# Runs of extra TensorE products behind the last contraction of a two-layer attention and MLP kernel

## The chip, the cores and the metric

The kernel runs on one core of a Trainium2 chip. A core has TensorE (PE in the profile; its loads of the stationary operand are listed as PEld), VectorE (DVE), ScalarE (ACT), GpSimd (POOL) and SyncE (SP), which run beside each other and wait for each other through semaphores. The metric is the device time of one execution, in microseconds, as the median of several runs. Less is better.

## The reference

Four layers in a row, each added to its input: linear attention, MLP, and both again with the same weights. There are 2048 tokens of 640 features.

```python
def _A_ref(x, wqkv, w_phi, wo):
    q, k, v = heads_of(x @ wqkv)                      # H = 32 heads, Dh = 20
    pq = jnp.einsum("bhsd,hdf->bhsf", q, w_phi)
    pk = jnp.einsum("bhsd,hdf->bhsf", k, w_phi)
    phi_q = jnp.concatenate([_softmax(pq), _softmax(-pq)], axis=-1)
    phi_k = jnp.concatenate([_softmax(pk), _softmax(-pk)], axis=-1)
    kv = jnp.einsum("bhsf,bhsd->bhfd", phi_k, v)
    z = jnp.einsum("bhsf->bhf", phi_k)
    o = (phi_q @ kv) / (phi_q . z + 1e-6)
    return o.reshape(B, S, D) @ wo

def _B_ref(x, w1, b1, w2):                            # 640 -> 1536 -> 640
    h = jnp.einsum("bsd,df->bsf", x, w1) + b1
    act = h * jnp.tanh(softplus(h))                   # mish
    return jnp.einsum("bsf,fd->bsd", act, w2)

x = A_x
x = x + _A_ref(_layernorm(x), A_wqkv, A_w_phi, A_wo)
x = x + _B_ref(_layernorm(x), B_w1, B_b1, B_w2)
x = x + _A_ref(_layernorm(x), A_wqkv, A_w_phi, A_wo)
x = x + _B_ref(_layernorm(x), B_w1, B_b1, B_w2)
```

## The kernel before

The tokens are cut into 8 blocks (`NB`) of 256, each two row tiles (`BT` = 2) of 128. Large products are done in float32r: each operand is split into a high part and a low part (names ending in `h` and `l`), and every product becomes three, high x high, high x low and low x high, which accumulate in PSUM. So each factor of a matrix product shows up as three products in the profile, at lines 364 (projections), 759 (first MLP weight) and 801 (second MLP weight). Plain float32 products are used where operands are not split: folding the feature map into the weights (`fold_part`, line 244), the key-value sums (line 436), the averages (line 637). Transposes go through TensorE as well (lines 89, 300 and 608), with the identity `ident`.

A layer has three parts. `attend_first` computes keys, values and queries per block; `attend_second` computes the averages, the output projection and the normalization for the MLP; `dense` is the MLP. The change touches `dense`, in its second and last call (`last` is true).

`dense` walks through 48 steps, 8 blocks times 6 pairs of 128-wide slices of the 1536 hidden features. `hidden` (lines 749 to 765) computes one pair: 30 products with a stationary operand of 128 x 128 from `w1s` and 256 moving columns, into a PSUM tile of the tag `one` (four buffers of 512 columns). `mish` (lines 767 to 785) turns the result into the activation on ScalarE, VectorE and GpSimd and splits it into `ah` and `al`; for the last step it does so in two halves. `contract` (lines 787 to 802) multiplies a pair with the second weight: 24 products with 128 stationary columns from `ah` or `al` and 320 moving columns (`HC` = 320), into PSUM tiles of the tag `mm`. It runs two steps behind `hidden` (`SKEW` = 2), so that the activation has time:

```python
for i in range(len(steps) + SKEW):
    if i < len(steps):
        ...
        acts[i] = hidden(b, pr)
    ...
    if i >= SKEW:
        b, pr = steps[i - SKEW]
        contract(b, pr, *acts.pop(i - SKEW))
        if pr == n_pr - 1:
            end(b)
```

`end` (lines 804 to 829) adds the residual on VectorE. For the last block of the last layer it does so in four pieces of 320 columns (line 811), and sends the output in three transfers from SyncE's queue (lines 813 and 815). Behind that stands only the closing of the program, which the profile puts down to line 959: waits for the engines and transfers, and two rounds in which the engines meet.

The order of each engine's queue comes from a planner that goes by the order of the program text and a simulated timeline; in `dense` nothing is ordered by hand except a few ScalarE instructions (`tc.issue_after`). Instructions of one engine run in the order of its queue. Waits between engines are put in by the framework from what each instruction reads and writes. The line `warm` at the start issues 30 transposes of the identity into a PSUM tile that is not read.

Of the kernel before, what the change touches and what calls it, by code (L numbers as in the profile page):

```python
# [16 lines left out]
P = 128  # L17
# [5 lines left out]
KD = D // P  # L23
# [10 lines left out]
SKEW = 2  # L34
# [7 lines left out]
def kernel(  # L42
# [13 lines left out]
    nc = tc.nc  # L56
# [8 lines left out]
    def mm_tile():  # L65
        return psum.tile([P, 2, 512], F32, tag="mm", name="mm", bufs=2)

    def one_tile():
        return psum.tile([P, 512], F32, tag="one", name="one", bufs=4)
# [10 lines left out]
    def row_block(t, b):  # L80
        return t[b * BLK:(b + 1) * BLK, :].rearrange("(p t) d -> p t d", t=BT)


    ident = const.tile([P, P], F32, name="ident")
# [98 lines left out]
    def load_v_weights():  # L183

        ws = [r1_pair(k) for k in range(KD)]
        for k in range(KD):
            split(ws[k][0][:, D:2 * D], ws[k][1][:, D:2 * D], fetch_v(k))
        return ws
# [77 lines left out]
    def norm_stats(t, xt):  # L266

        bn = work.tile([P, 2, 6], F32, tag="bn", name="bn", bufs=2)
        for c in range(2):
            nc.vector.bn_stats(bn[:, c], xt[:, t, c * HC:(c + 1) * HC])  # L270
        mv = work.tile([P, 2], F32, tag="mv", name="mv", bufs=3)
        nc.vector.bn_aggr(mv, bn)
        return mv

    def norm_scale(b, mvs):

        ve = work.tile([P, BT], F32, tag="ve", name="ve", bufs=2)
        for t in range(BT):
            nc.gpsimd.tensor_scalar(ve[:, t:t + 1], mvs[t][:, 1:2], LN_EPS, 1.0, op0=ALU.add, op1=ALU.mult)
        nc.gpsimd.tensor_tensor(stats[:, b, 0], ve, neg_half, op=ALU.pow)  # L280
        for t in range(BT):
            nc.vector.scalar_tensor_tensor(stats[:, b, 1, t:t + 1], mvs[t][:, 0:1], -1.0,
                                           stats[:, b, 0, t:t + 1], op0=ALU.mult, op1=ALU.mult)
# [32 lines left out]
    def row_tile():  # L316
        return work.tile([P, D], F32, tag="xn", name="xn", bufs=4)
# [9 lines left out]
    def normalize(b, dst, src):  # L327
        for t in range(BT):
            act(dst[t], src[t], AF.Identity, bias=stats[:, b, 1, t:t + 1], scale=stats[:, b, 0, t:t + 1])

    def spill_turned(rows, dst):

        dst = dst.rearrange("(j f) (t q s) -> t q f j s", f=32, t=BT, s=32)
        for t in range(BT):
            nc.vector.transpose(rows[t], rows[t])
            for q in range(4):
                nc.sync.dma_start(dst[t, q], rows[t][32 * q:32 * q + 32].rearrange("f (j s) -> f j s", s=32))

    def load_turned(src, tiles):

        cols = []
        for c, make in zip(range(0, KD, 2), tiles):
            n = min(2, KD - c)
            cols.append(make()[:, :n * BLK].rearrange("p (k s) -> p k s", k=n))
            nc.sync.dma_start(cols[-1], src[c * P:(c + n) * P].rearrange("(k p) s -> p k s", p=P))
        return Transposed(cols=cols)
# [55 lines left out]
    def fetch(x_src, b, xt=None):  # L402
        xt = x_tile() if xt is None else xt
        nc.sync.dma_start(xt, row_block(x_src, b))
        return xt
# [339 lines left out]
    def dense(x_src, x_dst, w1s, w2s, first, last):  # L745
# [41 lines left out]
        def contract(b, pr, ah, al):  # L787
            if pr == 0:
                blocks[b][2] = [mm_tile() for _ in range(BT)]
            pys = blocks[b][2]  # L790
            order = [(t, j) for t in range(BT) for j in range(2)]
            if b == NB - 1 and pr == KF // 2 - 1:
                order = [(t, j) for j in range(2) for t in range(BT)]
            for t, j in order:
                sl = slice(t * P, (t + 1) * P)
                f = 2 * pr + j
                for c in range(2):
                    cs = slice(c * HC, (c + 1) * HC)
                    wh, wl = w2s[f][0][:, cs], w2s[f][1][:, cs]
                    for n, (l, r) in enumerate(((ah, wh), (ah, wl), (al, wh))):  # L800
                        nc.tensor.matmul(pys[t][:, c, :HC], l[:, j, sl], r,  # L801
                                         start=(f == 0 and n == 0), stop=(f == KF - 1 and n == 2))

        def end(b):
            xt, _, pys = blocks.pop(b)
            dst = row_block(x_dst, b)
            if last and b == NB - 1:
                for t in range(BT):
                    for c in range(2):
                        cs = slice(c * HC, (c + 1) * HC)  # L810
                        nc.vector.tensor_tensor(xt[:, t, cs], pys[t][:, c, :HC], xt[:, t, cs], op=ALU.add)  # L811
                        if t == BT - 1:
                            nc.sync.dma_start(dst[:, t, cs], xt[:, t, cs])
                    if t < BT - 1:
                        nc.sync.dma_start(dst[:, t], xt[:, t])
                return
            mvs = []
            for t in range(BT):
                nc.vector.tensor_tensor(xt[:, t, :].rearrange("p (c d) -> p c d", c=2), pys[t][:, :, :HC],
                                        xt[:, t, :].rearrange("p (c d) -> p c d", c=2), op=ALU.add)  # L820
                if not last:
                    mvs.append(norm_stats(t, xt))
            if not last:
                norm_scale(b, mvs)
            nc.sync.dma_start(dst, xt)
            if not last:
                xn = [row_tile() for _ in range(BT)]
                normalize(b, xn, [xt[:, t, :] for t in range(BT)])
                spill_turned(xn, n2_d[b])

        ahead = [None] * BT

        def fetch_rows_of(b):
            for t in range(BT):
                ahead[t] = row_tile()
                nc.sync.dma_start(ahead[t], row_block(x_src, b)[:, t, :])
# [4 lines left out]
        acts = {}  # L841
        nxt = kv_ws = None
        for i in range(len(steps) + SKEW):
            if i < len(steps):
                b, pr = steps[i]
                if pr == 0 and b + 1 < NB:
                    fetch_rows_of(b + 1)
                if pr == 2 and b + 1 < NB:
                    blocks[b + 1] = [fetch(x_src, b + 1), None, None]
                if pr == 3 and (b + 1 < NB or not last):  # L850
                    nxt = load_turned(n1_d[b + 1] if b + 1 < NB else n2_d[0], (v_tile, v_tile, row_tile))
                acts[i] = hidden(b, pr)
                if pr == 1 and b + 1 < NB:
                    with tc.issue_after(exps[0]):
                        normalize(b + 1, ahead, ahead)
                    spill_turned(ahead, n1_d[b + 1])
                if b == 0 and pr == n_pr - 2:
                    with tc.issue_after(exps[0]):
                        nxt.step()
                if pr == n_pr - 1 and (b + 1 < NB or not last):  # L860
                    if b + 1 < NB:
                        blocks[b + 1][1] = nxt
                    with tc.issue_after(exps[0]):
                        nxt.all()
            if i <= KD:
                with tc.issue_after(exps[0]):
                    w = next(last_w2)
                if i:
                    w2s[6 + i] = w
            if i == len(steps) - 1 and not last:  # L870
                with tc.issue_after(exps[0]):
                    kv_ws = load_v_weights()
            if i >= SKEW:
                b, pr = steps[i - SKEW]
                contract(b, pr, *acts.pop(i - SKEW))
                if pr == n_pr - 1:
                    end(b)
        return nxt, kv_ws

    with tc.block(schedule_with_timeline_sim=True):  # L880
        src, first = x, None
        for layer in range(LAYERS):
            last = layer == LAYERS - 1
# [4 lines left out]
            w1s = []  # L888
# [29 lines left out]
            def begin_dense():  # L918
                return normed(0, x1t[0])

            begun = attend_second(src, x1_d, acc, [lambda s=s: fetch_step(*s) for s in steps],
                                  [lambda s=s: make_step(*s) for s in steps], fetch_dense, begin_dense)
            first = dense(x1_d, dst, w1s, w2s, [x1t[0], begun, None], last)
            src = dst

# [37 lines left out]
```

## Time and profile before

| | us |
|---|---|
| median of 2 runs | 1377.49 |
| lowest, highest | 1376.79, 1378.2 |
| span of the profiled execution, first to last instruction | 1375.0 |

The profile is one execution recorded by the hardware. Its page lists busy time by engine, the chain of work that ended last, and the costliest groups of instructions. A group reads: line, engine, operation, output <- inputs, shapes (for TensorE rows x stationary columns, then the moving operand), the count, then busy time in us and the mean ns of one record, then idle time before them with the releaser. A timeline row reads: start in us, length in us, engine, line, operation, and how many were merged. The records of products overlap, since one drains while the next streams.

The groups of the three large product lines and of the activation's slowest instruction:

```profile
L801 PE MATMUL mm<-r2h,ol 128*128 128x320 f32 x1280 | 305.0, 309 | 0.0
L785 POOL TENSOR_TENSOR ol<-big,ol 128x512 fp32r<-128x512 f32 (+1 forms) x98 | 129.9, 1326 | 483.7 <-ACT ol L784 409.3
L759 PE MATMUL one<-xtl,r1h 128*128 128x256 f32 x960 | 268.2, 279 | 0.0
...
L364 PE MATMUL mm<-r1h,xth 128*128 128x320 f32 x600 | 187.6, 313 | 1.6 <-DVE r1l L251 1.6
```

### The profile page before, as it was taken

How to read it: one execution, taken by the hardware profiler on the slowest of the kernel's cores; microseconds unless marked ns; L12 is line 12 of the kernel's file. 1: busy time of each engine (PE TensorE's matmuls, PEld its weight loads, DVE VectorE, ACT ScalarE, POOL GpSimd, SP SyncE). 2: the span in 40 equal slices, each digit the busy share in tenths (PEclk: the TensorE clock that was granted, in tenths of full speed). 3: DMA queues.
4: the chain of work that ended last, by engine and by line, in shares of the span. 5: the costliest groups of instructions: out<-in, count | busy, mean ns of one | idle time of the engine just before them, and what ended most of it. 6: DMA issues, size and time to landing. Idle time of an engine off the chain costs nothing.

```text
span 1375.0 us, 30860 instructions
## 1 busy us (share of the span) xinstructions
PE 1362.1 (99%) x12896; PEld 1349.8 (98%) x12896; DVE 1073.3 (78%) x1822; ACT 581.3 (42%) x970; POOL 441.0 (32%) x334
## 2 busy tenths in 40 slices
PE   9999999999999999999999999999999999999998
PEld 8999999999999999999999999999999999999998
DVE  5898877886688887788769899988678776677775
ACT  4344443222454545545444334332235444454443
POOL 1345553354322222122235434444242111111112
PEclk9999999999999999999999999999999999999999
DMA  9443424788614442244473433368975221333200
GB/s 337 148 95 62 75 40 96 204 242 292 224 55 97 116 105 77 59 107 99 141 245 77 85 59 64 67 132 270 285 253 151 77 59 41 94 97 96 69 29 20
DMA packets 350469, 169.85 MB, mean 124 GB/s; under 512 B 287209, under 2 KB 323801, under 8 KB 350329
## 3 DMA queue, kind: packets, MB, share of 16 engines
q1 hardware_dynamic: 350329, 167.88, 45.2%
q8 instruction: 101, 1.65, 0.5%
q14 instruction: 39, 0.32, 0.1%
HBM read 104.92 MB, written 62.91 MB: 122 GB/s over the span
## 4 chain that ended last, share of the span: by engine, by line
PE 96%; DMA 1%; DVE 1%; ACT 0%; issue 0%; DVEq 0%; SPq 0%
PE mm L364 29%; PE one L759 24%; PE mm L801 24%; PE one L364 12%; PE mm L637 3%; PE one L300 2%; PE one L436 2%; DMA v<-in_wv 1%; DMA r1l<-wp_d 0%; DVE r1l L251 0%; DVE bn L270 0%; ACT xn L129 0%; DVE r L397 0%; DVE xt L811 0%; ACT r L129 0%
## 5 line engine op out<-in xcount | busy, mean ns | idle before, releaser
L801 PE MATMUL mm<-r2h,ol 128*128 128x320 f32 x1280 | 305.0, 309 | 0.0
L785 POOL TENSOR_TENSOR ol<-big,ol 128x512 fp32r<-128x512 f32 (+1 forms) x98 | 129.9, 1326 | 483.7 <-ACT ol L784 409.3
L759 PE MATMUL one<-xtl,r1h 128*128 128x256 f32 x960 | 268.2, 279 | 0.0
L759 PE MATMUL one<-xth,r1l 128*128 128x256 f32 x960 | 268.0, 279 | 0.0
L759 PE MATMUL one<-xth,r1h 128*128 128x256 f32 x960 | 265.9, 279 | 0.0
L801 PEld LDWEIGHTS mm<-r2h,ol 128*128 128x128 f32 x1280 | 219.2, 188 | 0.3 <-ACT ol L784 0.3
L801 PE MATMUL mm<-r2l,ol 128*128 128x320 f32 x640 | 197.3, 309 | 0.0
L364 PE MATMUL mm<-r1h,xth 128*128 128x320 f32 x600 | 187.6, 313 | 1.6 <-DVE r1l L251 1.6
L364 PE MATMUL mm<-r1l,xth 128*128 128x320 f32 x600 | 185.8, 310 | 0.0
L364 PE MATMUL mm<-r1h,xtl 128*128 128x320 f32 x600 | 185.6, 310 | 0.0
L759 PEld LDWEIGHTS one<-xtl,r1h 128*128 128x128 f32 x960 | 180.4, 188 | 0.0
L759 PEld LDWEIGHTS one<-xth,r1l 128*128 128x128 f32 x960 | 180.4, 188 | 0.0
L759 PEld LDWEIGHTS one<-xth,r1h 128*128 128x128 f32 x960 | 179.6, 188 | 0.0
L774 DVE TENSOR_SCALAR big<-big 128x512 f32<-128x512 f32 (+1 forms) x98 | 57.1, 583 | 110.0 <-ACT big L772 109.8
L399 POOL TENSOR_TENSOR r<-r,r 128x1280 f32<-128x1280 f32 x32 | 77.7, 2429 | 156.4 <-DVE r L398 141.8
L801 PEld LDWEIGHTS mm<-r2l,ol 128*128 128x128 f32 x640 | 120.2, 188 | 0.0
L776 ACT ACTIVATE big<-big,two 128x512 f32<-128x512 f32 (+1 forms) x98 | 70.1, 716 | 116.1 <-DVE big L775 116.0
L772 ACT ACTIVATE big<-one,b1s 128x256 f32<-128x256 f32 x192 | 80.9, 468 | 89.0 <-PE one L759 88.5
L784 ACT ACTIVATE ol<-big 128x512 fp32r<-128x512 f32 (+1 forms) x98 | 60.9, 622 | 136.0 <-DVE big L783 135.9
L364 PEld LDWEIGHTS mm<-r1h,xth 128*128 128x128 f32 x600 | 112.8, 188 | 2.6 <-DVE r1l L251 1.8
L364 PEld LDWEIGHTS mm<-r1h,xtl 128*128 128x128 f32 x600 | 112.7, 188 | 0.2
L364 PEld LDWEIGHTS mm<-r1l,xth 128*128 128x128 f32 x600 | 112.8, 188 | 0.0
(133 smaller groups left out, 3119.9 us busy)
## 6 DMA issues: line engine op xcount, KB each, us to landing
e_d<-r SPq DMA_DIRECT2D x128, 160.0 KB, 4.0
big<-e_d SPq DMA_DIRECT2D x32, 640.0 KB, 7.6
x_d<-xt SPq DMA_DIRECT2D x23, 640.0 KB, 3.9
xt<-x_d SPq DMA_DIRECT2D x22, 640.0 KB, 5.5
n_d<-xn SPq DMA_DIRECT2D x176, 80.0 KB, 2.2
xt<-in_x SPq DMA_DIRECT2D x16, 640.0 KB, 4.4
xn<-x_d SPq DMA_DIRECT2D x28, 320.0 KB, 4.4
v<-n_d SPq DMA_DIRECT2D x30, 256.0 KB, 3.1
```

The lines of the kernel that those rows point to most:

```text
L300: nc.tensor.transpose(ps[:, c, t * P:(t + 1) * P], self.rows[t][:, (c0 + c) * P:(c0 + c + 1) * P], ident)
L364: nc.tensor.matmul(ps[:, :HC], a[:, sl], r, start=(k == 0 and n == 0), stop=(k == KD - 1 and n == 2))
L399: nc.gpsimd.tensor_tensor(eg, eg, r.unsqueeze(2).to_broadcast([P, 2 * H, DH]), op=ALU.mult)
L436: nc.tensor.matmul(kva[32 * j:32 * j + DH + 1, 40 * r:40 * r + 40], v[:, (DH + 1) * h:(DH + 1) * (h + 1)], e[:, 40 * h:40 * h + 40], start ...
L637: nc.tensor.matmul(po[64 * q:64 * q + 64, c, GW * j:GW * j + w], phs[g][:n, s0:s0 + 64], kvb[:n, g, :w], start=True, stop=True)
L759: nc.tensor.matmul(ph[:, j, :], l, r, start=(n == 0), stop=(n == 3 * KD - 1))
L772: exps[0] = nc.scalar.activation(part(ta, 0)[:, j - js.start], ph[:, j, :], AF.Exp, bias=b1s[:, 2 * pr + j:2 * pr + j + 1]).ins
L774: nc.vector.tensor_scalar_min(e, e, E_CAP)
L776: nc.scalar.activation(r, n, AF.Ln, bias=two)
L784: nc.scalar.activation(ah[:, js], n, AF.Copy)
L785: nc.gpsimd.tensor_tensor(al[:, js], n, ah[:, js].bitcast(F32), op=ALU.subtract)
L801: nc.tensor.matmul(pys[t][:, c, :HC], l[:, j, sl], r, start=(f == 0 and n == 0), stop=(f == KF - 1 and n == 2))
```

## The change

A new function `widths` in `dense` issues 168 products on TensorE; it is called once, behind the loop, in the last layer. It takes `ah` and `al` of the last step, 128 columns of either as the stationary operand (`sides`), and columns from 512 on of the first MLP weight as the moving operand. It writes two PSUM tiles of the tag `one`. Nothing reads them, and the output is what it was. `contract` gets the same operands as before through two names.

```diff
+        def widths(ah, al):
+
+            ps = [one_tile() for _ in range(2)]
+            sides = (ah[:, 0, :P], al[:, 0, :P], ah[:, 1, :P], al[:, 1, :P])
+            for w in (512, 480, 384, 320, 256, 192, 128, 64):
+                for n in range(12):
+                    nc.tensor.matmul(ps[0][:, :w], sides[n % 4], w1s[n % KD][n % 2][:, 512:512 + w],
+                                     start=(n == 0), stop=(n == 11))
+            for n in range(12):
+                nc.tensor.matmul(ps[1][:, :320], sides[0], w1s[n % KD][n % 2][:, 512:832],
+                                 start=(n == 0), stop=(n == 11))
+            for n in range(12):
+                nc.tensor.matmul(ps[1][:64, :320], sides[n % 4][:, :64], w1s[n % KD][n % 2][:, 512:832],
+                                 start=(n == 0), stop=(n == 11))
+            for n in range(12):
+                nc.tensor.matmul(ps[1][:32, :320], sides[n % 4][:, :32], w1s[n % KD][n % 2][:, 512:832],
+                                 start=(n == 0), stop=(n == 11))
+            for n in range(12):
+                nc.tensor.matmul(ps[n % 2][:, :320], sides[n % 4], w1s[n % KD][n % 2][:, 512:832],
+                                 start=True, stop=True)
+            for n in range(12):
+                nc.tensor.matmul(ps[0][:, :64], ident, ident[:, 64 * (n % 2):64 * (n % 2) + 64],
+                                 start=(n == 0), stop=(n == 11))
+            for n in range(12):
+                nc.tensor.matmul(ps[0][:, :128], ident, ident, start=(n == 0), stop=(n == 11))
...
-                contract(b, pr, *acts.pop(i - SKEW))
+                ah, al = acts.pop(i - SKEW)
+                contract(b, pr, ah, al)
                 if pr == n_pr - 1:
                     end(b)
+        if last:
+            widths(ah, al)
         return nxt, kv_ws
```

So there are eight runs of 12 products with 512, 480, 384, 320, 256, 192, 128 and 64 moving columns; then four runs of 12 at 320 columns, one with a single stationary operand, one with 64 stationary columns, one with 32, and one in which every product starts and ends its own sum; and two runs of 12 in plain float32 with the identity as both operands, at 64 and at 128 columns.

## The prediction

> **What bounds the kernel now.** I read the page first: the span, the busy shares and the chain of work that ended last.
>
> ```profile
> span 1375.0 us, 30860 instructions
> PE 1362.1 (99%) x12896; PEld 1349.8 (98%) x12896; DVE 1073.3 (78%) x1822; ACT 581.3 (42%) x970; POOL 441.0 (32%) x334
> ...
> PE 96%; DMA 1%; DVE 1%; ACT 0%; issue 0%; DVEq 0%; SPq 0%
> ```
>
> TensorE is busy for 99% of the span and carries 96% of the chain. The change adds work at one place only, so next I read the chain in order of time over the last 46 us; these are its last pieces.
>
> ```profile
> 1352.87 3.52 PE mm L801 x24
> 1356.39 3.50 PE one L759 x30
> 1359.89 9.99 PE mm L801 x68
> 1369.88 0.02 issue
> 1369.90 0.89 DVE xt L811 x2
> 1370.79 0.40 DVEq L959
> 1371.18 0.40 DVE xt L811
> ```
>
> Products are issued without a gap to the end. The 68 of the last contraction take 9.99 us, 146.9 ns each; the 24 before them 3.52 us, 146.7 ns. The 30 products 256 wide take 3.50 us, 116.7 ns. These prices are from start to start. A record is longer than that (0.31 us for a product 320 wide, below), because one product drains while the next streams, so a sum of records would count the time twice.
>
> Last comes the tail, in the timeline of the final 5 us and in the view of the closing instructions (line 959, with their first and last start).
>
> ```profile
> 1369.90 1.69 DVE L811 TENSOR_TENSOR xt<-mm,xt 128x320 f32<-128x320 f32 x4 [3.53 <-PE mm L801]
> ...
> 1370.14 0.31 PE L801 MATMUL mm<-r2h,ol 128*128 128x320 f32 x1
> 1370.82 0.34 SPq L815 DMA_DIRECT2D out<-xt  x1
> 1371.21 0.92 SPq L813 DMA_DIRECT2D out<-xt  x2
> ```
>
> ```profile
> L959 SPq EVENT_SEMAPHORE  x7: 17/28/28, 1373.9 to 1374.9; - x7
> ```
>
> TensorE's last product starts at 1370.14 and ends at 1370.45. Then VectorE adds the residual, three transfers go out, SyncE's first closing wait is over at 1373.9, and the kernel ends 1.1 us later, at 1375.0. So TensorE is idle for the last 4.55 us. The profiled span is 1375.0 us; the median of the two runs is 1377.49 us, 2.49 us more, which lie outside the first and last instruction. I carry a difference of spans over to the median unchanged.
>
> **The change, part by part.** Nothing is removed, and no transfer, VectorE or ScalarE work is added. The diff adds, behind the last contraction, 12 products for each of eight widths (96), then four runs of 12 that are 320 wide (48), all with float32r operands, and 24 products of plain float32 (12 at 64 columns, 12 at 128). They read `ah` and `al` of the last step, the first MLP weight and the identity, all of which lie in SBUF by then. They write two tiles of the tag `one`, which nobody reads. No new wait for another engine arises: the last reader of `one` tiles is the last activation, which the last contraction needs anyway. They stand behind the contraction on TensorE's queue, so neither the residual adds nor the output transfers wait for them. What they cost is TensorE's time, minus what the tail hides.
>
> Widths 512 to 256: 146.7 ns at 320 columns and 116.7 ns at 256 are 0.458 and 0.456 ns a column. I take 0.458. The widths 512, 480, 384, 320 and 256 are 1952 columns: 894 ns for one product of each. A straight line through the two points would give 898 ns, which changes the sum by 0.05 us.
>
> Widths 192, 128 and 64: The trace has no float32r product below 256 columns. Below some width the product no longer hides the load of the next stationary operand. What a load costs is seen where plain float32 products are narrow (timeline of the weight folding), and in the weight loads grouped by shape:
>
> ```profile
> 31.72 0.83 PE L244 MATMUL mm<-big,raw 120*128 120x120 f32 x6
> 32.39 0.83 PE L244 MATMUL one<-big,raw 120*128 120x120 f32 x6
> 33.06 0.58 PE L244 MATMUL mm<-big,raw 120*128 120x120 f32 x4
> 33.47 0.39 PE L244 MATMUL mm<-big,r 80*128 80x80 f32 x2
> 33.70 0.61 PE L244 MATMUL one<-big,raw 120*128 120x120 f32 x4
> ```
>
> ```profile
> L801 PEld LDWEIGHTS mm<-r2h,ol 128*128 128x128 f32 x1280 | 219.2, 188 | 0.3 <-ACT ol L784 0.3
> ...
> L759 PEld LDWEIGHTS one<-xtl,r1h 128*128 128x128 f32 x960 | 180.4, 188 | 0.0
> ...
> L759 PEld LDWEIGHTS one<-xth,r1h 128*128 128x128 f32 x960 | 179.6, 188 | 0.0
> ...
> L637 PEld LDWEIGHTS mm<-kvb,big 120*64 120x64 f32 x1280 | 40.0, 138 | 3.9 <-PE one L300 1.7 <-PE mm L637 1.0 <-issue 0.8
> ...
> L436 PEld LDWEIGHTS one<-big,v 128*21 128x21 f32 x2048 | 21.8, 101 | 4.0 <-issue 3.3 <-POOL r L389 0.8
> L244 PEld LDWEIGHTS mm<-big,raw 120*128 120x128 f32 x48 | 6.1, 191 | 2.5 <-DMA raw<-in_wqk_t 1.1 <-DVE r1l L251 1.1 <-issue 0.4
> ```
>
> Six records 120 wide take 0.67 us (31.72 to 32.39, and again to 33.06), 112 ns each; two that are only 80 wide take 0.23 us, 115 ns each. A third fewer columns bring nothing: this is a floor, and it is the load of 128 stationary columns. The load records agree in size: 138 ns for 64 columns and 188 to 191 ns for 128, so 64 columns more cost 50 to 53 ns, and 128 some 100 to 106 ns. The float32r loads (L801, L759) take 188 ns, the same as plain float32 (191 ns), so I give float32r the same floor: 112 ns for each of the widths 192, 128 and 64, 336 ns together. Lower bound: no floor, 0.458 ns a column, 384 columns, 176 ns together. Upper bound: the price of a plain float32 product, in the rivals. All eight widths cost 894 + 336 = 1230 ns, twelve times 14.76 us.
>
> The Trainium skill (TensorE: Matmul & The Clock Gate, section Back-to-back issue gap) gives the distance of warm products as N / 2.4 + 2.5 ns with a lowest value near 25 ns, and no floor from the load. By it the eight widths would take an estimated 11.9 us instead of 14.76. The trace differs from it at 320 columns: 146.7 ns against the estimate of 135.8.
>
> Four runs of 320: Each product keeps its 320 columns, so 146.7 ns: 48 of them, 7.04 us. With 64 or 32 stationary columns the load is shorter, and it was hidden already. One stationary operand for twelve products saves nothing, because L759 shows it: the products with `xth` and `xtl` share one stationary operand (`r1h`) and follow each other, yet each has its own load, 960 and 960. Were that load left out, nothing would be gained either, since it is hidden. A product that starts and ends its own sum costs as one that accumulates. Bounds: 2.7 us more, if the 24 loads with few columns were not hidden and each cost a full 112 ns. None of it less, since the stream of 320 columns remains. I take zero, since the 128-column loads of L801 (1280 in the row above) are hidden behind products of just this width.
>
> Plain float32: A product becomes two records here. L436 has 2048 of them for 32 heads x 16 row tiles x 2 layers = 1024 products. Each record costs at least the load, 112 ns. A stream of 128 columns fits under it, as the transposes show:
>
> ```profile
> 1017.30 1.25 PE L300 MATMUL one<-ident,xn 128*128 128x128 f32 x10
> ```
>
> (1.25 - 0.27) / 9 = 109 ns, taking 0.27 us as one record. So both widths cost 2 x 112 ns: 24 products, 48 records, 5.38 us. Lower bound: 64 columns stream in 54 ns, if their loads were hidden: 1.4 us less.
>
> Sum: 14.76 + 7.04 + 5.38 = 27.18 us on TensorE. The slot behind the last contraction opens at 1370.14 + 0.147 = 1370.29. The last record starts one slot (0.112) before 1397.47, at 1397.36, and ends 0.275 us later (the length of a 112 ns record in the timeline: 0.83 - 5 x 0.112), at 1397.63. The residual adds and the output transfers, over at 1373.9, lie wholly under the new products. The closing then waits for TensorE and not for the transfers: at most the 1.1 us it took before, less the waits that are met already; I take 1.0. Span 1398.6, 23.6 us more than 1375.0. Forecast: 1377.49 + 23.6 = 1401.1 us, 1.7% slower. The clock stays as it is: the last contraction ran at the full granted clock (1.00), and the added products leave no gap in which it could fall.
>
> ```profile
> 1359.89:1369.88 9.99, 9.99 (x70) 9.99 (x70) 5.11 (x12) 3.54 (x8) 2.47 (x3) 1.00 0.01 2
> ```
>
> The cover is 4.55 us of TensorE's idle time at the end, of which 1.0 us returns as closing. Without it the change would cost the whole 27.2 us, 2.0%.
>
> **The rivals.**
>
> Narrow float32r goes at the price of plain float32: The place is the widths below 256 columns. For it: the kernel shows float32r at 256 and 320 columns only, never below. Against it: whether an instruction is one record or two is fixed when the program is built, and float32r is one record everywhere. Price: two records each, at 112 ns for 64 and 128, and at 192 columns a stream of 192 x 109 / 128 = 164 ns, 327 ns a product. That is 327 + 224 + 224 = 775 instead of 336 ns, 5.3 us more in all: 1406.4 us, slower by 2.1%. It decides the sign from 3.9 us more than my sum on, for 2% of 1377.49 is 27.5 us, which is about what a measurement of this kernel can tell from no change. A weaker form, one record that takes twice the transposes' time a column (2 x 0.85 ns: 327, 218 and, by the load, 112 ns), costs 3.9 us more, 1405.0, just on that bound. I give both 13%.
>
> No floor: loads are hidden below 256 columns too: For it: 128-column loads vanish wholly at 256 and 320 columns. Against it: the 112 and 115 ns above. Then the three widths cost 176 ns, 1.9 us less: 1399.2; with the 64-column float32 products also at their stream, 1397.8. I give it 12%. The Trainium skill (same page, section Weight-path perf modes) says that a fast weight load acts on 128 weights whose type is not FP32, which would be such a case if float32r did not count as FP32. The trace speaks against that here, with the equal 188 and 191 ns.
>
> The products are dropped, because nobody reads them: Then nothing changes: 1377.5. Against it stand 30 products at the start that nobody reads either and that are all in the trace:
>
> ```profile
> L89 PE MATMUL one<-ident 128*128 128x128 f32 x30 | 5.1, 350 | 1.3 <-POOL ident masks.py:199 1.3
> ```
>
> I give it 2%. The planner could also put some of them earlier, in a gap of TensorE; since the first four need the last `ah` and `al`, at most a few could move, and a product costs the same time on a full queue wherever it stands.
>
> **How the numbers follow.** The forecast, 1401.1 us, has 73%, with a range of its own from 1399.5 to 1403.5 (1.4 us less for float32 at 64 columns, most of the 2.7 us more for unhidden loads). The rivals have 13, 12 and 2%. The range 1398 to 1406.5 leaves out only the dropped products and the far ends. Faster by over 2% has no mechanism: 1%. Slower by over 2% needs 1405.0: the first rival in its stronger form, part of the weaker one, and unhidden loads on top of something else: 12%. Within 2%: 87%.
>
> **What would show it.** The chain of waits should end in TensorE's new lines, and the closing should follow them by about 1 us; the output transfers should land over 20 us before the end. In the timeline, twelve products should take 2.8 us at 512 columns, 1.76 at 320, 1.4 at 256, and 1.34 at each of 192, 128 and 64. If the times fall below 256 with the width, there is no floor; if 192 takes 2.6 us or more, the first rival holds, and two records for one product would prove its stronger form. The two plain float32 runs should be 24 records each in 2.7 us, alike at 64 and 128. The runs with 64 and 32 stationary columns should equal the 320 run; a longer one would mean loads that aren't hidden. The forecast is wrong if earlier stages differ in their order by more than the 1 us by which runs differ, or if the granted clock falls in the added stretch.

## The result, and the profile after

The changed kernel takes 1400.66 us in the median of two runs (1399.2 and 1402.12), against 1377.49 before: a ratio of 1.0162 with a 95% interval from 1.0125 to 1.0199. The forecast was 1401.1. As a difference from the kernel before, the two medians give 23.2 us, and 23.6 were forecast. The page of the profiled execution, which is the run of 1402.12 us, shows TensorE's work grown by 28.7 us and the other engines' unchanged (VectorE 1073.3 before, 1074.2 after):

```profile
span 1400.3 us, 31244 instructions
PE 1390.8 (99%) x13088; PEld 1377.2 (98%) x13088; DVE 1074.2 (77%) x1822; ACT 581.3 (42%) x970; POOL 441.4 (32%) x334
```

TensorE has 192 more records: 144 products in float32r with one each and 24 in plain float32 with two each. The chain of waits, in order of time, near the last contraction (the rest of it is the new lines):

```profile
1358.35 3.50 PE one L759 x30
1361.85 7.63 PE mm L801 x52
1369.48 0.23 PE one L837
1369.70 1.46 PE one L840 x10
...
```

Two things are to be seen here. First, the last 30 products of line 759 start at 1358.35 and not at 1356.39 as before, so 1.96 us of the longer span arose before any added product ran. From that point to the end it is 1400.3 - 1358.35 = 41.95 us, against 1375.0 - 1356.39 = 18.61 before: the change itself costs 23.3 us. Second, the planner did not leave all of the new products behind the contraction. One of 512 columns and ten of the run with a single stationary operand stand between its 52nd and 53rd product.

The timeline gives the price of each run, as the distance between the first products of one run and the next; the run of 512 columns is taken from its second product behind the contraction (line 837 is the run of widths; line, stationary columns and moving columns are in each row):

```profile
1374.17 0.39 PE L837 MATMUL one<-r1h,ol 128*128 128x512 f32 x1
...
1376.49 0.38 PE L837 MATMUL one<-r1h,ol 128*128 128x480 f32 x1
...
1379.14 0.34 PE L837 MATMUL one<-r1h,ol 128*128 128x384 f32 x1
...
1381.23 0.31 PE L837 MATMUL one<-r1h,ol 128*128 128x320 f32 x1
...
1382.99 0.28 PE L837 MATMUL one<-r1h,ol 128*128 128x256 f32 x1
...
1384.41 0.25 PE L837 MATMUL one<-r1h,ol 128*128 128x192 f32 x1
...
1385.73 0.24 PE L837 MATMUL one<-r1h,ol 128*128 128x128 f32 x1
...
1387.04 0.24 PE L837 MATMUL one<-r1h,ol 128*128 128x64 f32 x1
...
1388.35 0.39 PE L840 MATMUL one<-r1h,ol 128*128 128x320 f32 x1
```

| moving columns | us for the run | ns a product | forecast, ns |
|---|---|---|---|
| 512 | 2.32 for 10 | 232 | 235 |
| 480 | 2.65 | 221 | 220 |
| 384 | 2.09 | 174 | 176 |
| 320 | 1.76 | 147 | 147 |
| 256 | 1.42 | 118 | 117 |
| 192 | 1.32 | 110 | 112 |
| 128 | 1.31 | 109 | 112 |
| 64 | 1.31 | 109 | 112 |

Down to 256 columns a product costs its width, and from 192 down it costs the same. The three last values are somewhat low because the first distance in such a run is only 79 to 86 ns; this returns at the next wide product, where the first distance is 0.22 us, at 1388.35. Inside these runs the distance is 112 ns.

The other 1.96 us lie for the most part in the middle of the program. The wait between the two layers, near 702 us, is also in the kernel before. In this execution it is 0.87 and 0.64 us long (brackets: idle time before, and what ended it):

```profile
702.60 0.41 PE L801 MATMUL mm<-r2h,ol 128*128 128x320 f32 x1 [0.87 <-ACT ol L784]
...
704.10 0.71 PE L364 MATMUL one<-r1h,xth 128*128 128x320 f32 x3 [0.64 <-ACT r1h L137]
```

After it, the view of stretches (busy time of each engine with records in brackets, then TensorE's granted clock) shows a lower clock from 704.5 to 708.5 us. In the changed kernel:

```profile
704.50:708.50 4.00, 4.00 (x19) 4.00 (x18) 3.64 (x7) 1.09 (x2) 1.55 (x1) 0.57 0.20 49
```

The same stretch in the kernel before:

```profile
704.50:708.50 4.00, 4.00 (x29) 4.00 (x28) 4.00 (x10) 0.76 (x2) 1.57 (x1) 1.00 0.47 140
```

A mean of 0.57 over 4 us fits 3.4 us at 0.5. TensorE issued 19 records there instead of 29, ten fewer at 147 ns, 1.5 us; the rest of the 1.96 us are waits that are a few tenths longer. Up to the 53rd product of the last contraction the queues of all engines hold the same instructions in the same order in both kernels.

### The profile page after: what moved, and what is told of

It is laid out like the page before. It is cut to its first block, busy times and chain, and to the rows that moved or that the text cites. A ratio compares the mean times of both kernels' runs of the same rounds, so it can differ in the third digit from the quotient of the medians.

```text
span 1400.3 us, 31244 instructions
## 1 busy us (share of the span) xinstructions
PE 1390.8 (99%) x13088; PEld 1377.2 (98%) x13088; DVE 1074.2 (77%) x1822; ACT 581.3 (42%) x970; POOL 441.4 (32%) x334
## 4 chain that ended last, share of the span: by engine, by line
PE 96%; DVE 1%; DMA 0%; ACT 0%; issue 0%; DVEq 0%; ACTq 0%
PE mm L364 28%; PE one L759 24%; PE mm L801 24%; PE one L364 11%; PE mm L637 3%; PE one L300 2%; PE one L436 2%; PE one L837 1%; DMA v<-in_wv 0%; PE one L855 0%; DVE r1l L251 0%; PE one L852 0%; DVE bn L270 0%; PE one L840 0%; PE one L849 0%
```

## The experiments

Each is the changed kernel with one edit, unless it says otherwise. Since executions of one kernel differ by up to 5 us, the chip's median is given with its interval, and beside it a second measure from the profile that leaves out whatever happened earlier: the time from the start of the last 30 products of line 759 to the end of the span. It was 18.61 us before and 41.95 after.

**The changed kernel again.** No edit.

> The changed kernel once more, unaltered, to settle its distance from the kernel before. The added products take 27.09 us on TensorE in its first profile, 3.7 us of it lie in time in which TensorE was idle anyway. Theory A (products by the row prices, minus the cover; the slip of 2.0 us in the middle of the first profile, where the granted clock was 0.5 for 3.4 us, is a matter of the single run): 23.4 us over before, between 22 and 24, and the kernel before shows runs with such a slip as well. Theory B (the slip comes with the change): 25.3 us over before in nearly all runs.

Median of five runs 1403.01 us (1399.95 to 1403.73), against 1377.95 for 15 runs of the kernel before; ratio 1.0177 (1.0163 to 1.0191), 25.1 us. In the profile, a run of 1399.95 us, the last part starts at 1356.18 and the span is 1398.2: 42.0 us, the same as in the first profile. This profile holds no records of the granted clock, so that a 1.00 in its views says nothing; but TensorE has 29 records from 704.5 to 708.5 us, as in the kernel before, so the slow stretch is not there. So the end of the kernel repeats to a tenth of a microsecond, and the run to run difference lies earlier. The mean granted clock that is recorded with each run points the same way: of the seven runs of the changed kernel, the four with 0.999 took 1402.1 to 1403.7 us and the three with 1.0, this one among them, took 1399.2 to 1400.8 (a stretch of 3.4 us at 0.5 lowers the mean by 0.0012). The median fits theory B, the fastest runs theory A; this run alone does not decide between them.

**All of it behind the contraction.** `done[0]` is the last product that `contract` issued.

```diff
-            widths(ah, al)
+            with tc.issue_after(done[0].ins):
+                widths(ah, al)
```

> All added products are held behind the last product of the contraction; in the first profile the planner had put 11 of them, 1.7 us, into the contraction. Theory A (a product costs the same wherever it stands on a full queue, and the residual adds and output transfers are under cover either way): the same time as the changed kernel within 0.5 us, while the residual adds and transfers start 1.7 us earlier. Rival (their place in the contraction cost or saved time): 1.7 us away from it.

Median of four runs 1400.29 us (1399.19 to 1400.66); ratio 1.0158 (1.0144 to 1.0172). Its chain of waits:

```profile
1356.55 3.50 PE one L759 x30
1360.05 10.56 PE mm L801 x72
1370.61 14.63 PE one L837 x96
1385.24 1.84 PE one L840 x12
1387.08 1.73 PE one L843 x12
1388.82 1.74 PE one L846 x12
1390.56 1.76 PE one L849 x12
1392.33 2.62 PE one L852 x24
1394.95 2.73 PE one L855 x24
```

The contraction runs through in 10.56 us, and its end is at 14.1 us after the start of line 759's last products, 1.7 us earlier than in the changed kernel. The end of the kernel is unmoved: 1398.5 - 1356.55 = 41.95 us. So the planner's placing cost nothing and saved nothing, as theory A has it. The two medians, 1400.29 here and 1403.01 for the changed kernel, do differ by 2.7 us; that lies ahead of the last part, where one of these four runs has a mean clock of 0.999 and three of those five do. These rows also give the other runs: 144 ns a product with 64 stationary columns (line 843), 145 with 32 (line 846), 147 when each product starts and ends its own sum (line 849), 109 and 114 ns a record in plain float32 at 64 and 128 columns (112 inside both runs). The sum of the seven rows of added products is 27.05 us.

**Plain float32 alone.** The runs in float32r are left out, the rest stands behind the contraction.

```diff
-            for w in (512, 480, 384, 320, 256, 192, 128, 64):
...
+            with tc.issue_after(done[0].ins):
+                widths(ah, al)
```

> Of the added products only the 24 in plain float32 are kept, 5.4 us of TensorE's time, held behind the contraction. Theory A (the tail covers 3.7 us): 1.7 us over before, the span ends 0.84 us behind the last product. Rival (no cover, every added product lengthens the kernel in full): 5.4 us over before. Rival (cover of the whole idle 4.55 us): 0.8 us over.

Median of eleven runs 1378.93 us (1377.42 to 1381.95); ratio 1.0011 (1.0002 to 1.0019), 1.0 us. In its profile (span 1377.0 us):

```profile
1356.79 3.50 PE one L759 x30
...
1370.85 2.62 PE one L835 x24
1373.48 2.73 PE one L838 x24
```

From 1356.79 to 1377.0 it is 20.2 us, 1.6 more than before, for 5.35 us of products. So 3.7 us were covered by the tail; no cover at all would have been 5.4. The chip's median, 1.0 with an interval from 0.3 to 2.6 us, also excludes that, and leaves the 0.8 us of the third theory open; the profile's 1.6 decides for theory A.

**Ahead of the last contraction.** The products run before the last call of `contract`, with the activation of the step before.

```diff
+                if last and i == len(steps) + SKEW - 1:
+                    with tc.issue_after(done[0].ins):
+                        widths(ah, al)
                 ah, al = acts.pop(i - SKEW)
...
-        if last:
-            widths(ah, al)
```

> The same 168 products stand ahead of the last contraction, with the activation of the step before as the stationary operand, so that the residual adds and the output transfers follow them as they follow the contraction before. Theory A (the cover is the tail): the full 27.1 us over before, 3.7 us more than the changed kernel. Rival (the end is set by TensorE's sum alone): the same as the changed kernel within 0.5 us.

Median of four runs 1403.53 us (1402.72 to 1406.12); ratio 1.0186 (1.0172 to 1.02), 25.6 us. In the profile (span 1404.3 us) the contraction comes last again, with the tail behind it:

```profile
1358.95 3.50 PE one L759 x30
...
1396.56 2.66 PE mm L801 x18
...
```

From 1358.95 to 1404.3 it is 45.35 us, 26.7 more than before, for 27.1 us of products, and 3.4 more than in the changed kernel. On the chip it is 3.2 us over the run with all products behind the contraction, but only 0.5 over the median of the changed kernel (1403.01), which by itself would fit the rival; the lowest runs, 1402.72 and 1399.95, are 2.8 us apart. The last part of the profile, free of what differs earlier, decides for theory A. So the same products cost 23.3 us behind the contraction and 26.7 ahead of it: the cover is the tail. Of the expected 27.1 us 0.3 are missing; by the profile they are in the closing, behind TensorE's last product.

**What the floor is.** The 14 runs give way to runs with fewer stationary columns.

```diff
+            for m in (128, 96, 64, 32):
+                for w in (128, 64):
+                    for n in range(24):
+                        nc.tensor.matmul(ps[0][:m, :w], sides[n % 4][:, :m], w1s[n % KD][n % 2][:, 512:512 + w],
+                                         start=(n == 0), stop=(n == 23))
...
```

> In place of the 14 runs of the change stand runs of 24 float32r products with 128, 96, 64 and 32 stationary columns, at 128 and at 64 moving columns, then one at 64 with a single stationary operand, and two of plain float32 at 64 moving columns with 64 and 32 stationary columns, all behind the contraction. Theory A (the floor of 112 ns is the load of 128 stationary columns, 0.87 ns a column): 112 ns with 128, 84 with 96, 56 to 59 with 64, and with 32 the stream, 58 ns at 128 and 29 at 64 moving columns; 112 with the single stationary operand, since it is loaded again each time; plain float32 56 ns a record. Span about 18 us over before. Rival (a floor of every product narrower than 256, whatever is stationary): 112 ns in all, plain float32 112 a record, span about 30 us over before.

One run, 1403.94 us, span 1402.2: 27 us over before, near neither theory. The timeline and the view of stretches say why. The rows of each pair below are the same kind of product, 10, 10 and 14 products apart:

```profile
1376.00 0.25 PE L838 MATMUL one<-r1l,ol 128*96 128x128 f32 x1
...
1376.85 0.25 PE L838 MATMUL one<-r1l,ol 128*96 128x128 f32 x1
...
1377.06 0.36 PE L838 MATMUL one<-r1l,ol 128*96 128x128 f32 x1
...
1378.66 0.36 PE L838 MATMUL one<-r1l,ol 128*96 128x128 f32 x1
...
1390.68 0.19 PE L838 MATMUL one<-r1h,ol 128*32 128x64 f32 x1
...
1391.13 0.19 PE L838 MATMUL one<-r1h,ol 128*32 128x64 f32 x1
```

The run with a single stationary operand, in the chain of waits:

```profile
1391.36 2.68 PE one L841 x24
```

The view of stretches, where the granted clock is the third figure from the end:

```profile
1377.00:1380.40 3.40, 3.40 (x25) 3.40 (x23) 0.00 (x0) 0.00 (x0) 0.00 (x0) 0.50 0.00 0
```

With 96 stationary columns a product takes 85 ns at full clock, against 112 with 128: the floor goes with the stationary columns, 0.87 to 0.89 ns for each, as theory A says. With 32 stationary and 64 moving columns it is 32 ns, about the 29 of the stream. With a single stationary operand (line 841) it is 112 ns again, so the load is done each time. The rival, one floor for all narrow products, falls. But near 1377 us the granted clock went to 0.5, the product of 96 columns went from 85 to 160 ns, and those of 64 ran at 107 ns; at full clock they were not seen, and half of 107 would be 53. The plain float32 records took 58 ns with 64 stationary columns and 56 with 32 once the clock was back, near the 56 expected. Neither theory had the fall of the clock, and TensorE had been busy without a gap.

**The type.** Runs of 24 products at five widths, in bfloat16 (copies of the activation and of one weight, made by VectorE) and in float32r.

```diff
+            for w in (512, 320, 256, 128, 64):
+                for n in range(24):
+                    nc.tensor.matmul(ps[0][:, :w], b16[:, n % 4], w16[:, :w], start=(n == 0), stop=(n == 23))
...
```

> In place of the change's runs stand runs of 24 products of 512, 320, 256, 128 and 64 moving columns with 128 stationary columns, once with bfloat16 operands (made from the last activation and the first MLP weight by VectorE), once with float32r, all behind the contraction. float32r as in the change: 233, 147, 118, 112, 112 ns. Theory A (the floor is the load, and its length goes with the bytes of the stationary operand): bfloat16 at 64 and 128 columns falls clearly under 112 ns, to about 56. Rival (the load goes by the column, whatever the type): 112 ns for bfloat16 as well. For the wide products: if the 0.453 to 0.458 ns a column belong to the four-byte type, bfloat16 is under 0.43 ns a column at 512; if they belong to the array, the same 233 and 147 ns.

One run, 1404.22 us. The groups by shape (count, then busy us, in which overlaps count once, and mean ns of a record); line 841 is bfloat16, line 844 float32r:

```profile
L844 PE MATMUL one<-r1h,ol 128*128 128x320 f32 x24 | 3.7, 309 | 0.0
L841 PE MATMUL one<-big 128*128 128x320 bf16 x24 | 3.4, 299 | 0.0
...
L841 PE MATMUL one<-big 128*128 128x128 bf16 x24 | 1.5, 219 | 0.0
L841 PE MATMUL one<-big 128*128 128x64 bf16 x24 | 0.9, 193 | 0.0
```

The weight loads of the same two lines:

```profile
L844 PEld LDWEIGHTS one<-r1h,ol 128*128 128x128 f32 x120 | 16.3, 190 | 1.1
L841 PEld LDWEIGHTS <-big 128*128 128x128 bf16 x120 | 9.1, 98 | 4.1
```

The distance is the busy time less one record, over 23. In bfloat16 that is (1.5 - 0.219) / 23 = 56 ns at 128 columns and 31 ns at 64 (29 between the starts of single records), far below 112: the floor is the load of a four-byte operand, whose record is 190 ns long against 98. Theory A had about 56 at both widths; since 64 columns take about half of that, a bfloat16 load costs at most 29 ns, less than half of 112, and its length does not simply go with the bytes. At 320 columns bfloat16 takes (3.4 - 0.299) / 23 = 135 ns and float32r 147, so the higher price of a column belongs to the type too. The rule N / 2.4 + 2.5 ns of the Trainium skill (TensorE: Matmul & The Clock Gate, section Back-to-back issue gap), from which the trace of the kernel before differed, gives estimates of 55.8 and 135.8 ns for 128 and 320 columns: bfloat16 here agrees with it, and float32r does not go by it. The section calls this the gap of an isolated product without a budget for loads, and says that in a stream of load and product pairs both set the distance, with 81 ns at 128 columns; the bfloat16 pairs here took 56. The fast weight load of the Trainium skill (the same page, section Weight-path perf modes) is for types that are not FP32; the short loads of bfloat16 agree with that, and float32r does not get it.

**Narrow products for longer.** To see what lowered the clock: 72 products at 192, 128 and 64 moving columns, always 128 stationary ones, with 48 products of 320 after each.

```diff
+            for w in (192, 128, 64):
+                for n in range(72):
+                    nc.tensor.matmul(ps[0][:, :w], sides[n % 4], w1s[n % KD][n % 2][:, 512:512 + w],
+                                     start=(n == 0), stop=(n == 71))
+                for n in range(48):
+                    nc.tensor.matmul(ps[1][:, :320], sides[n % 4], w1s[n % KD][n % 2][:, 512:832],
+                                     start=(n == 0), stop=(n == 47))
```

> In place of the change's runs stand three runs of 72 float32r products with 128 stationary columns, at 192, 128 and 64 moving columns (8.0 us each at 112 ns), each followed by 48 products of 320 columns (7.0 us), all behind the contraction. In e5_columns the granted clock fell to 0.5 although the products followed each other without a gap. Theory A (the clock follows how large a share of the time the array streams; with 64 moving columns that is 27 of 112 ns): it falls in the run of 64, probably not in the run of 192, and comes back in the products of 320; in the run of 64 the distance becomes about 213 ns, 2.8 us or more are added, and the span is 50 us or more over before. Rival (it fell because of the fewer stationary columns, 96 and less): the clock stays at 1.00 throughout, 112 ns in all three runs, 41.5 us over before in the span.

One run, 1424.89 us, span 1423.1 (48 us over before, where theory A had 50 or more and the rival 41.5). The chain of waits:

```profile
1370.64 8.02 PE one L837 x72
1378.65 7.07 PE one L840 x48
...
1400.80 12.24 PE one L837 x72
1413.04 9.23 PE one L840 x48
```

The view of stretches from the start of the run of 64 columns:

```profile
1400.60:1403.90 3.30, 3.30 (x32) 3.30 (x31) 0.00 (x0) 0.00 (x0) 0.00 (x0) 1.00 0.00 0
1403.90:1412.80 8.90, 8.90 (x44) 8.90 (x44) 0.00 (x0) 0.00 (x0) 0.00 (x0) 0.50 0.00 0
1412.80:1417.60 4.80, 4.80 (x20) 4.80 (x20) 0.00 (x0) 0.00 (x0) 0.00 (x0) 0.50 0.00 0
```

At 192 moving columns the 72 products take 8.02 us, 111 ns each, at full clock, and at 128 it is 7.99 us. At 64 the clock falls 3.3 us after the run began, and the run takes 12.24 us; the wide products behind it still lose 2 us before the clock is back. The stationary columns are the same throughout, so the rival falls. Only the moving columns differ, and with them how much of the time the array streams.

The traces show a second thing, which the expectations did not have: the clock changes in steps. Eleven of the thirteen profiles hold records of the granted clock, and in each of them it changes only at whole multiples of 3.413 us behind its first rise, which comes 4.1 to 7.3 us after the start and differs from run to run. Here the fall is 410 steps behind the rise, and the step that ends with it began at 1400.52, just ahead of the run of 64 columns. So the 3.3 us are what this run fills of one step, and the clock came back at the end of the first step that the wide products filled. An estimate of the streaming in each step, from its records and their prices here (0.458 ns a moving column in float32r, 0.42 in bfloat16, 0.87 for a record of plain float32), fits theory A in all eleven: ahead of each of the seven falls that come before the end of the products, the array streams for 27 to 43% of the step, and in the steps at full clock without a fall for 43% or more, but for one of 39% at the end of e7_before. The Trainium skill (TensorE: Matmul & The Clock Gate, section The HAM clock gate) says that a monitor sets the clock by how busy the array has been in windows of about 3.4 us, and warns of idle gaps; the steps of 3.413 us agree with that, and this run shows such a fall without any gap in TensorE's records.

**The slip in the middle, in the kernel before.** Four more profiles of the kernel before, unaltered.

> The kernel before, unaltered, for its profile. Theory A (the stretch of granted clock 0.5 near 705 us is a matter of the single run and not of the change): it shows up in some profile of the kernel before too, with the same 3.4 us and some 1.7 us of cost, where the wait between the two layers near 702 us happens to be longer. Theory B (it comes with the change): never here.

> The kernel before a second time, for the same question, with the same expectations.

> The kernel before once more, for its profile, on the same question as e7_before: whether the stretch of granted clock 0.5 near 705 us shows up without the change. Theory A: it does in some runs, with a span of 1377 us or more. Theory B: it never does.

> The kernel before once more, for the same question, with the same expectations.

The runs took 1377.09, 1376.94, 1377.83 and 1376.56 us, and their spans are 1374.7 to 1376.1, so none reached the 1377 of theory A. In none of them does the clock fall near 705 us. In e8_before there is such a stretch of 3.4 us near 36 us, behind another wait, and in e5_columns there is one at the same place. So the fall near 705 was never seen in five profiles of the kernel before, and in two of eight profiles of kernels with added products (the first one and e4_ahead), where the instructions up to that point are the same. That is too few to tell theory A from B by counting.

Two things on record speak for theory A. Six of the 15 runs of the unaltered kernel beside e1_again have a mean granted clock of 0.998 or 0.997. That is an estimated 4 us or more at 0.5, while at the end of its five profiles it was at most 1.6 us; so these runs had such a stretch ahead of the end, and where it lay is not on record. And the steps of 3.413 us give a reason why it comes in one execution and not in another. In the first profile of the changed kernel both waits near 702 us lie in one step:

```profile
701.38:704.79 3.41, 1.90 (x11) 1.37 (x10) 1.40 (x3) 1.83 (x3) 0.73 (x1) 1.00 0.70 243
704.79:708.20 3.41, 3.41 (x15) 3.41 (x14) 3.05 (x6) 0.80 (x2) 1.55 (x1) 0.50 0.17 35
```

By the estimate above the array streams for 39% of this step, and for 43% of its like in e4_ahead; in the other nine profiles with a clock record it is 56% or more in every step near 702 us. In e6_bf16 TensorE waits longer there, 1.68 us against 1.51, but a step ends within the first wait, at 702.42, and the clock stays. So it takes a long wait and a step that lies badly, and both vary from run to run. Whether added products make that wait longer more often was not settled.

## Why the prediction was right

Its steps, in its order:

- The prices of the wide products, read as 0.458 ns a column from 320 and 256, held: 232, 221, 174, 147 and 118 ns against 235, 220, 176, 147 and 117.
- The floor of 112 ns for narrow float32r products, taken from plain float32 products and from load records of the same length, held; it is the load of 128 stationary columns, as the runs with 96 and 32 columns and with bfloat16 showed. The upper rival (the price of plain float32) would have needed two records for a product or 327 ns at 192 columns; there was one record and 110 ns. The lower rival (no floor) holds for bfloat16, not here.
- The four runs at 320 columns: 7.07 us by the four rows of the run with all products behind the contraction, against 7.04. Loads with few columns stay hidden; the 2.7 us kept as a bound were not needed. A single stationary operand saved nothing.
- Plain float32: 5.35 us against 5.38.
- The sum: 27.05 against 27.18 us. The closing behind the last product, taken as 1.0 us, was 0.84, so the cover is 3.7 us instead of 3.55. Together that makes 23.3 us against 23.6. One reading of the sum was off without effect: the 2.49 us between span and median do not all lie outside the first and last instruction, since the median is that of two runs; the profiled run itself took 1376.79 us, 1.79 more than its span.
- The products were all executed, so the third rival falls.

Two steps were not right, and neither changed the number. That at most a few products could move ahead, because the first four need the last `ah` and `al`: eleven moved, ten of them from the run at line 840, which needs only a quarter of these operands and has a PSUM tile of its own. The run with all products behind the contraction shows that this cost nothing. And that the clock stays up because the added products leave no gap: it stayed up, but the missing gap is not why. In e9_long_narrow products of 64 columns pulled the clock down without a gap; in the change their run is 1.3 us long and fills no step of 3.413 us.

The profiled span grew by 25.3 us and not by 23.3, through the 1.96 us in the middle of the program. That the two-run median came so near the forecast is in part luck: the two runs are 2.9 us apart, one above and one below it, and five more runs put the change at 25.1 us, 1.5 over the forecast difference. The prediction took 1 us as what runs differ by; 15 runs of the kernel before reach from 1376.12 to 1380.68.

## What to carry to other kernels

Price a product on TensorE by the distance to the next one, as the larger of its stream and the load of its stationary operand: for float32r here some 0.46 ns a moving column and 0.87 ns a stationary column, so that with 128 stationary columns nothing is gained by going below about 240 moving columns (an estimate from these two prices). Of work that is added behind the last use of an engine the tail covers a part, here 3.7 us of 4.55 with 5.35 us added and with 27.05; the rest costs in full, and so does work ahead of it. For differences of a few microseconds in a long kernel, compare a stretch of the profile that begins behind the part that varies from run to run.

## What the runs showed that was not expected

TensorE's granted clock fell to 0.5 while its records followed each other without a gap. With 64 moving and 128 stationary columns it did so 3.3 us after the run began, the distance of the products went from 112 to about 213 ns, and it recovered only some 4.5 us into wide products. With 128 or 192 moving columns it did not fall within 8.0 us. So a load that cannot be hidden cost twice here: it set the pace, and where it left the array streaming for some 43% of a step of 3.413 us or less (the estimate above), the clock fell.

float32r streams about 8% slower than bfloat16 at the same granted clock (147 against 135 ns at 320 columns), also with 64 or 32 stationary columns (144 and 145 ns), so it is not the load. In e9_long_narrow the products of 320 columns took 267 ns while the clock was at 0.50, which is less than twice 147, so that the price does not simply go with the granted clock. What it is was not tried.
